# Low parts of the attention's probabilities and of X moved between VectorE and GpSimd, and one accumulating transfer issued later

## The chip, the core and the metric
One core of one Trainium2 chip runs the whole program. The metric is the device time of one execution in microseconds; smaller is better. The core's engines work from queues of their own, each in program order: TensorE (PE; PEld is its weight loads), VectorE (DVE), ScalarE (ACT), GpSimd (POOL) and SyncE (SP), which here only issues transfers.

## What is computed
Attention over 4 x 8 = 32 heads of 768 tokens and 64 columns, with a mask: a query sees only the keys whose six sign bits under a random projection equal its own. Then a mixture of eight experts over the 3072 tokens, each expert taking at most 384.

```python
q_bits = (einsum('bhsd,dk->bhsk', q, proj) > 0); k_bits = ...
mask = q_bucket[:, :, :, None] == k_bucket[:, :, None, :]
scores = np.where(mask, scale * q @ k.T, -1e9)
attn = softmax(scores);  x = attn @ v          # [4*768, 8*64]
logits = x @ w_gate                            # greedy assignment, cap N // E
out[mask_e] = np.maximum(x[mask_e] @ w1[e], 0.0) @ w2[e]
```

## The kernel before
Products run on 16-bit operands. A number is therefore split into a high part (a cast) and a low part (the number minus its high part), and a product is the sum of three: high x high, high x low, low x high. Much of the work beside TensorE is making these low parts.

The 32 heads come in eight groups of four (h = 4G + j). A group's q, k and v are loaded at once (L77). ScalarE casts the high parts (`cast`). For groups 3 to 7 the low part of q and k is made by ScalarE writing the negated high part (`turn`, L152) and a GpSimd transfer that adds the f32 original from DRAM to it (`adds`, L154). SP then moves the parts into the operand tiles QA, KA, QB, KB (`moves`, L200, signs L206).

The main loop runs over steps t, six for each head (one for each block of 128 keys), and in each step emits its parts in the order of `ORD='SF0r1LRA'`: S the score passes of a head some twelve steps ahead, for its row maxima (TensorE L267, VectorE reduction L269); F the last key block's product with v and the quotient `norm` (L353 to L357, tile X); 0 and 1 the two halves of a block's scores and exponentials (`ST`, TensorE L316 and L317, ScalarE L318, tile pt); L the low part of the probabilities of the step before (`lo`, L322 for one block, L325 for two at once); A the product with v (`AV`, L339 to L341); r and R whatever was put by `add(n, ...)` on half-step n = 2t (r) or 2t + 1 (R). The product `AV` of block s of head h stands four steps behind its scores (`LAG=4`).

Who makes `lo` is chosen by head: `E0` for head 0, `E1` for head 1, else the list of the head in `EL`, else `PAT[h % 2]`. A number below 6 in the list gives that block to VectorE; 10, 11 or 12 gives the first, second or third pair of blocks to VectorE as one instruction (11: third and fourth key block). All else goes to GpSimd.

When two heads (an odd h and the one before) are done, their 128 columns X are stored as f16 high and low parts (tile XS): `xhigh` on ScalarE (L365) at half-step 12h + 23, `xlow` (L367) four half-steps later, that is in step 6h + 13, the second step of head h + 2, behind that step's `lo`. `xlow` also calls `xout`, which issues on SP a turning transfer XS to XT (L377) and one to x_dram (L378).

Other work with a fixed place: v's high part by ScalarE and low part `vl` by VectorE (`sv`, L221, two instructions in steps 4 and 5 of the second head of a group); a head's maxima are copied by VectorE (`m_four`, L277, at the end of a step), turned by TensorE two steps later (`m_turn`, L282), rectified by ScalarE (tile mr) and put into QA by a transfer on ScalarE's queue (`m_lay`, L287, qa<-mr), which the head's scores L316 need. TensorE's L231 sums v for the rows that no key matches.

`Z4` holds the half-steps of groups 4 to 7 relative to 48(G - 1): four `turn` (q, k, q, k) and then the two `adds` (q, k).

Of the kernel before, what the change touches and what calls it, by code (L numbers as in the profile page):

```python
# [15 lines left out]
PS = bass.MemoryType.PSUM  # L16
DR = bass.MemoryType.DRAM

AP=dict(PAT=[[11], []],
 ORD='SF0r1LRA',  # L20
 LAG=4,
 VM=[2, 2, 2, 2],
# [2 lines left out]
 E0=[3, 5],  # L25
 E1=[],
 X=[5, 4, 20, 15],
 XE=0,
 MR=3,
 MT=4,  # L30
 LEAD=[9,12,40,4],
# [9 lines left out]
 MS=74,  # L41
 BS=3,
 Z3=[77,85,88,91,93,97],
 Z4=[-20,-12,-18,-9,-15,-6],
 EA=[262, 32, 5],
 EG={2: 0, 3: 3},
 MO=['', 'AKs', 'BqL', 'lmk', 'c|ABqKLslmk', 'ABKLsq|cklm', 'ABKLsq|cklm'],
# [4 lines left out]
 OPS='i2 b0 t0 w6 r0 r2 k1 l0 l1 s0 r1 s1 c0 s2 P0 c1 g0 B0 D0 d0 u0 u1 f0 w2 s3 t1 C0 C1 m0 v0 e0 s4 w2 e1 s5 w2 e2 m1 r3 r5 l3 l2 v1 v2 s6 s7 | s8 | x0 | w0 | x1 s9 | r4 s10 | | | s11 m2 v3 | x3 | | x2 | m3 | | | | | |')  # L52
PAT,E0,E1,DW,LEAD=(AP[k] for k in ('PAT','E0','E1','DW','LEAD'))
NB=dict(S=2,T=3,V=1)
HK=385
EMPTY=60000.0
def attention(tc, nc, ctx, qT, kT, vv, proj, wg, x_dram, L, jp, identf, ident, B, late=None, after=None):
    S=768; NG=2*B; NH=8*B; LAG=AP['LAG']
    cp=ctx.enter_context(tc.tile_pool(name="cp",bufs=1))
# [4 lines left out]
    V=nc.vector; A=nc.scalar; G_=nc.gpsimd; T=nc.tensor; SY=nc.sync  # L64
# [129 lines left out]
    def moves(G,part=0):  # L194
# [15 lines left out]
        todo=dict(A=(go,QA,h[0]),B=(go,QB,h[0]),K=(go,KA,h[1]),L=(go,KB,h[1],64),s=(signs_,),c=(clear,G),q=(nxt,0),k=(nxt,1),l=(go,KB,l[1]),m=(go,QB,l[0],64))  # L210
        for x in AP['MO'][part] if G==1 else AP['MO'][min(G+2,6)].split('|')[part]:
            f,*x=todo[x]; f(*x)
# [134 lines left out]
    X={}; XS={}; normed=set(); turned={}  # L347
# [54 lines left out]
    def add(n,f,*a):  # L402
        if n>=2*(6*NH+LAG+6): raise ValueError('an operation has no step')
        at.setdefault(n,[]).append((f,a))
# [8 lines left out]
    n=-1; early=[]  # L413
    for o in AP['OPS'].split():
        if o=='|': n+=1
        elif n<0: OPS[o[0]](int(o[1:]))
        else: add(n,OPS[o[0]],int(o[1:]))
        if o[0]=='e': early.append(int(o[1:]))
    add(AP['WS'],wsplit); add(AP['SU'],sumv,0)
    for G in range(1,NG):  # L420
        p=AP['P1'] if G==1 else AP['P2'] if G==2 else AP['P3'] if G==3 else [48*(G-1)+x for x in AP['P4']]
        st,sg=(AP['P4'] if G>3 else p)[16:18]
# [3 lines left out]
        for n in range(4):  # L426
            if G<3: add(p[8+n],sub,G,n%2,n//2)
            else:
                z=AP['Z3'] if G==3 else [48*(G-1)+x for x in AP['Z4']]
                add(z[n],turn,G,n%2,n//2)  # L430
# [7 lines left out]
        for j in range(4):  # L438
            n=48*(G-1)+AP['CV'][j] if G>3 else p[15]+st*j
# [13 lines left out]
    for h in range(1,NH,2):  # L453
        b,d=h//8,h%8//2; n=2*(6*h+5+LAG)+AP['X'][0]
        if h==NH-1: n=2*(6*h+5+AP['LL'][5])
        if h==NH-1:
            for c in (0,3): add(n,xpart,4*b+d,1,c,c+3)
            for hf in range(2): add(n+AP['X'][1]*hf,xtr,b,d,hf)
            add(n+4,logits,b,[d]); add(n-5,xpart,4*b+d,0)
            add(n,xout,4*b+d,False)  # L460
        else:
            add(n,xhigh,4*b+d); add(n+AP['X'][1],xlow,4*b+d,(V,G_)[AP['XE']])
        if h==NH-1: pass
        elif b==B-1: add(n+AP['X'][3],logits,b,[d])
        elif d==3: add(n+AP['X'][2],logits,b,range(4))
        if after and d==3 and b in AP['EG']:
            for i,f in enumerate(after(AP['EG'][b],b,lambda: psT.tile([128,512],F32,name="pst"),lambda: psV.tile([128,512],F32,name="psv"))):
                add(n+5 if b==B-1 else max(n+AP['X'][2]+3,AP['EA'][0]+AP['EA'][1]*b)+AP['EA'][2]*i,f)
    for n,f in enumerate(late or ()):
        a,d=AP['LT'] if n<3 else AP['L0']  # L470
# [529 lines left out]
@with_exitstack  # L1000
def tile_bucket_attention_moe(ctx, tc, qT, kT, vv, proj, wg, w1, w2, out):
    nc = tc.nc
    B = qT.shape[0] // 2
    drp = ctx.enter_context(tc.tile_pool(name="drp", bufs=1, space=DR))
    x_dram = drp.tile([768 * B, 1024], F16, name="x_dram")
    M = Moe(tc, nc, ctx, 768 * B)
    late = M.consts()
    with ExitStack() as c1:
        c1.enter_context(tc.manual_schedule())
        attention(tc, nc, c1, qT, kT, vv, proj, wg, x_dram, M.Lm, M.jp, M.identf, M.ident, B, late, M.early)  # L1010
    with ExitStack() as c2:
        M.open(c2, x_dram, w1, w2, out)
        with tc.manual_schedule():
            M.start()
            M.run()
# [34 lines left out]
```

## Time and profile before
| | us |
|---|---|
| median of 3 runs | 702.49 |
| lowest and highest | 700.73, 705.22 |
| the profiled execution | 705.62 |
| its span, first to last instruction | 703.8 |

The profiled execution is one of its own; its rows are times inside the span. The attention fills the first 376 us or so, the routing and the experts the rest. In the rows, "out<-in" are the tiles written and read, "x" is a count, and a wait is put down to what ended it.

### The profile page before, as it was taken

To read this page: it belongs to the slowest core of one execution; us is meant where nothing else is said; L and a number is where in the kernel's file an instruction comes from. 1 tells how busy PE (TensorE), PEld (TensorE's weight loads), DVE (VectorE), ACT (ScalarE), POOL (GpSimd) and SP (SyncE) were. 2 spreads that over 40 slices of the span, in tenths; PEclk is the share of its full clock that TensorE was granted. 3 is DMA by queue.
4 is the path that set the end of the run, shared out by engine and by line. 5 is a ranking of instruction groups with operands and counts; after the bars stand their busy time and mean duration, and the time that the engine had idled before them with its cause. 6 is when DMAs were issued, how large, how long until landed. Compare 5 with 4: busy or idle time off the path is not lost. (4 is left out here: it accounts for less than half of the span.)

```text
span 703.8 us, 19016 instructions
## 1 busy us (share of the span) xinstructions
PE 656.3 (93%) x7761; PEld 420.3 (60%) x7769; DVE 525.7 (75%) x1226; ACT 393.8 (56%) x805; POOL 508.6 (72%) x464
## 2 busy tenths in 40 slices
PE   9899999899998999999996699999999999999994
PEld 2566676667666677677775565555555555555551
DVE  5879898778879779798887849798979797923110
ACT  5767787676777868765571253617171625353620
POOL 7599888777798678867840453858787878787751
PEclk9999999999999999999997599999999999999998
DMA  9539867778987789861122444353544445263501
GB/s 224 149 108 196 214 185 132 183 135 155 223 132 178 137 154 226 138 143 14 45 54 56 129 158 165 135 195 136 182 148 152 163 135 195 89 256 127 203 31 45
DMA packets 64300, 102.55 MB, mean 146 GB/s; under 512 B 28960, under 2 KB 53588, under 8 KB 62164
## 3 DMA queue, kind: packets, MB, share of 16 engines
q1 hardware_dynamic: 55236, 51.10, 32.0%
q0 software_dynamic: 8224, 50.08, 23.8%
q8 instruction: 61, 1.00, 0.6%
q10 hardware_dynamic: 752, 0.15, 0.1%
q14 instruction: 27, 0.22, 0.1%
HBM read 67.39 MB, written 12.58 MB: 114 GB/s over the span
## 5 line engine op out<-in xcount | busy, mean ns | idle before, releaser
L322 POOL TENSOR_TENSOR lo<-pt 128x768 f16<-128x768 f32 x148 | 245.1, 1674 | 41.9 <-ACT pt L318 37.3
L318 ACT ACTIVATE pt<-pst 128x384 f32<-128x384 f32 x384 | 173.3, 491 | 86.9 <-PE pst L317 82.2
L269 DVE TENSOR_REDUCE m<-pss 128x1 f16<-128x770 f32 x192 | 181.1, 956 | 34.1 <-PE pss L267 33.1
L316 PE MATMUL pst<-qa,ka 128*128 128x384 f16 x384 | 125.2, 326 | 9.4 <-DMA qa<-mr 4.7
L339 PE MATMUL psv<-vh,pt 128*128 128x65 f16 x1152 | 124.8, 195 | 1.6 <-DVE X L357 1.6
L341 PE MATMUL psv<-vh,lo 128*128 128x65 f16 x1152 | 124.6, 194 | 0.8 <-POOL lo L322 0.6
L317 PE MATMUL pst<-qb,kb 128*128 128x384 f16 x384 | 125.2, 326 | 0.0
L340 PE MATMUL psv<-vl,pt 128*128 128x64 f16 x1152 | 124.8, 193 | 0.0
L339 PEld LDWEIGHTS <-pt 128*128 128x128 bf16 x1152 | 107.4, 98 | 18.2 <-DVE X L357 3.7
L340 PEld LDWEIGHTS <-pt 128*128 128x128 bf16 x1152 | 106.2, 99 | 11.0 <-issue 0.2
L867 ACT CAST wh<-wf 128x1024 f16<-128x1024 f32 x64 | 65.4, 1042 | 77.6 <-DMA wf<-in_w_dram,zwidx 56.6
L341 PEld LDWEIGHTS <-lo 128*128 128x128 f16 x1152 | 106.3, 98 | 1.2 <-POOL lo L322 0.9
L267 PE MATMUL pss<-ka,qa 128*128 128x385 f16 x384 | 95.5, 333 | 4.0 <-DVE m L269 2.8
L879 POOL TENSOR_TENSOR wl<-wf,wh 128x512 bf16<-128x512 f32 x74 | 84.1, 1151 | 0.0
L902 PEld LDWEIGHTS <-wh 128*128 128x128 f16 x544 | 50.6, 99 | 30.4 <-issue 0.7
L858 POOL DMA_INDIRECT wf<-in_w_dram,zwidx x20 | 20.0, 998 | 57.2 <-DVE zmi L791 30.6
L914 PEld LDWEIGHTS <-hh 128*128 128x128 f16 x384 | 35.5, 98 | 36.2
L902 PE MATMUL ph<-xx,wh 128*128 128x384 f16 (+1 forms) x304 | 56.9, 313 | 0.0
L316 PEld LDWEIGHTS <-ka 128*128 128x128 f16 x384 | 37.7, 98 | 29.2 <-DMA qa<-mr 6.0
L317 PEld LDWEIGHTS <-kb 128*128 128x128 f16 x384 | 37.4, 97 | 27.4 <-issue 7.1
L902 PE MATMUL po<-xx,wh 128*128 128x384 f16 x240 | 48.1, 326 | 0.0
L989 POOL TENSOR_TENSOR wl<-wf,wh 128x512 bf16<-128x512 f32 x36 | 42.6, 1212 | 4.3 <-ACT wh L867 4.1
(292 smaller groups left out, 1217.6 us busy)
## 6 DMA issues: line engine op xcount, KB each, us to landing
vp<-in_vv_dram SPq DMA_DIRECT2D x8, 768.0 KB
x_dram<-XS SPq DMA_DIRECT2D x16, 384.0 KB
qp<-in_qT_dram SPq DMA_DIRECT2D x7, 768.0 KB
kp<-in_kT_dram SPq DMA_DIRECT2D x7, 768.0 KB
qa<-qh SPq DMA_DIRECT2D x14, 192.0 KB
ka<-kh SPq DMA_DIRECT2D x14, 192.0 KB
qb<-qh SPq DMA_DIRECT2D x14, 192.0 KB
kb<-kh SPq DMA_DIRECT2D x14, 192.0 KB
```

The lines of the kernel that those rows point to most:

```text
L267: T.matmul(ps[:,hf,0:HK],QA[u][:,j,qc*128:qc*128+128],KA[u][:,j,hf*HK:hf*HK+HK],start=True,stop=True)
L269: V.tensor_reduce(M6[h][:,qc:qc+1],ps[:,:,0:HK],axis=AX.XY,op=ALU.max,negate=True)
L316: T.matmul(ps[:,0:384],KA[u][:,j,kr],QA[u][:,j,r],start=True,stop=False)
L317: T.matmul(ps[:,0:384],KB[u][:,j,kr],QB[u][:,j,r],start=False,stop=True)
L318: A.activation(PT[h,kc][0][:,r],ps[:,0:384],AF.Exp,scale=0.125)
L322: eng.tensor_tensor(l,p,p.bitcast(BF)[:,1::2],op=ALU.subtract)
L339: T.matmul(av[:,c,:],ph[:,r],VH[u][:,j,kc,:],start=(kc==0 and c==0),stop=False,skip_group_check=True)
L340: T.matmul(av[:,c,0:64],ph[:,r],VL[u][:,j,kc,:],start=False,stop=False,skip_group_check=True)
L341: T.matmul(av[:,c,:],l[:,r],VH[u][:,j,kc,:],start=False,stop=False,skip_group_check=True)
L867: s.nc.scalar.copy(h[:,r],f[:,r])
L879: for _ in range(n): s.nc.gpsimd.tensor_tensor(*s.pend.pop(0)[1],op=ALU.subtract)
L902: T.matmul(p[:,r],a[:,o:o+128],b[:,d,r],start=n==0 and not c,stop=n==11 and c in (None,2),skip_group_check=c is not None)
```

## The change
Three edits. `PAT` gets the pair of the third and fourth key block also for odd heads (those without a list in `EL`: 9, 11, 13, 15, 17, 19, 21). `XE`, before the index of one engine for all heads (0: VectorE), becomes a range: `xlow` of heads 9 to 25 goes to GpSimd. The fifth number of `Z4`, q's `adds`, goes from -15 to -12.

```diff
-AP=dict(PAT=[[11], []],
+AP=dict(PAT=[[11], [11]],
- XE=0,
+ XE=[9,25],
- Z4=[-20,-12,-18,-9,-15,-6],
+ Z4=[-20,-12,-18,-9,-12,-6],
@@ the attention's list of operations
-            add(n,xhigh,4*b+d); add(n+AP['X'][1],xlow,4*b+d,(V,G_)[AP['XE']])
+            add(n,xhigh,4*b+d); add(n+AP['X'][1],xlow,4*b+d,G_ if AP['XE'][0]<=h<=AP['XE'][1] else V)
```

## Rows read from the trace of the kernel before
**Rows 1.** The page, part 1: busy us (share of the span) xinstructions.
```profile
PE 656.3 (93%) x7761; PEld 420.3 (60%) x7769; DVE 525.7 (75%) x1226; ACT 393.8 (56%) x805; POOL 508.6 (72%) x464
```
**Rows 2.** Stretches: length, each engine's busy us (x), granted clock, DMA share, GB/s.
```profile
120.00:130.00 10.00, 7.91 (x122) 5.67 (x119) 7.60 (x11) 5.07 (x12) 6.31 (x7) 0.95 0.79 156
130.00:140.00 10.00, 10.00 (x138) 7.14 (x137) 8.04 (x10) 7.23 (x18) 7.18 (x7) 0.87 0.80 213
...
130.00:345.00 215.00, 206.10 (x3258) 149.69 (x3257) 181.28 (x247) 153.47 (x356) 170.49 (x131) 0.99 0.76 148
```
**Rows 3.** Waits, 130 to 345 us: us in total, times, longest.
```profile
POOL lo L322 <- ACT pt L318: 28.0, 27, 3.0
...
POOL ql L154 <- ACT ql L152: 13.5, 4, 4.3
...
PE pst L316 <- ACT pt L318: 3.7, 4, 0.9
...
PE pst L316 <- DMA qa<-mr: 2.6, 2, 1.5
...
PE psv L339 <- DVE X L357: 1.4, 4, 0.4
...
PE pst L282 <- DVE m L277: 0.6, 2, 0.4
```
**Rows 4.** Timeline of GpSimd in head 10: start, us, instruction, [idle before <-releaser].
```profile
148.52 0.88 POOL L154 DMA_DIRECT2D ql<-in_qT_dram  x1 [2.77 <-ACT ql L152]
...
150.27 3.97 POOL L322 TENSOR_TENSOR lo<-pt 128x768 f16<-128x768 f32 x2 [0.75 <-ACT pt L318]
```
**Rows 5.** Instructions of tiles lo and XS: duration ns min/median/max, first and last start.
```profile
L322 POOL TENSOR_TENSOR lo<-pt x148: 1455/1467/3085, 28.4 to 360.2; 128x768 f16<-128x768 f32 x148
L325 DVE TENSOR_TENSOR lo<-pt x16: 1745/1748/2937, 54.7 to 369.6; 128x1536 f16<-128x1536 f32 x16
...
L367 DVE TENSOR_TENSOR XS<-X,XS x15: 946/1047/2254, 62.0 to 366.1; 128x768 f16<-128x768 f32 x15
```
**Rows 6.** Timeline of VectorE in head 17.
```profile
219.48 2.20 DVE L367 TENSOR_TENSOR XS<-X,XS 128x768 f16<-128x768 f32 x1
...
223.34 0.15 DVE L353 TENSOR_SCALAR r<-psv 128x6 f32<-128x6 f32 x1
...
225.09 1.64 DVE L221 TENSOR_TENSOR vl<-vp,vh 128x768 f16<-128x768 f32 x1
...
228.79 0.15 DVE L277 COPY m<-m 128x18 f16<-128x18 f16 x1
```
**Rows 7.** Timeline of TensorE: heads 8 and 9, head 17, head 21.
```profile
128.23 0.34 PE L316 MATMUL pst<-qa,ka 128*128 128x384 f16 x1 [2.09 <-DMA qa<-mr]
...
141.63 0.23 PE L282 MATMUL pst<-ident,m 128*128 128x128 f16 x1 [0.40 <-DVE m L277]
...
222.05 0.35 PE L346 MATMUL psv<-wf,qa 128*128 128x65 f16 x6
...
224.36 0.20 PE L339 MATMUL psv<-vh,pt 128*128 128x65 f16 x1 [0.34 <-DVE X L357]
...
228.42 0.34 PE L316 MATMUL pst<-qa,ka 128*128 128x384 f16 x1 [1.49 <-DMA qa<-mr]
...
230.29 0.22 PE L282 MATMUL pst<-ident,m 128*128 128x128 f16 x1
...
274.25 0.23 PE L282 MATMUL pst<-ident,m 128*128 128x128 f16 x1 [0.21 <-DVE m L277]
```
**Rows 8.** Timeline of SP, the next group's moves in head 11.
```profile
159.86 3.58 SPq L200 DMA_DIRECT2D qa<-qh  x2
163.49 1.28 SPq L200 DMA_DIRECT2D qb<-qh  x2
```
**Rows 9.** Timeline of VectorE in head 9.
```profile
137.30 2.06 DVE L221 TENSOR_TENSOR vl<-vp,vh 128x768 f16<-128x768 f32 x1
```

## Prediction
> **What bounds the kernel now.** Read the page's busy table first: TensorE works 93% of the span and no other engine more than 75% [rows 1]. The table by stretches says where the change can act: its edits touch heads 9 to 27, which run from about 130 to 345 us, and there TensorE is busy 206.1 of 215.0 us [rows 2]. So 8.9 us is all that could be won; the routing and expert stages behind 345 us only move along. The waits of that stretch then name the 8.9 us [rows 3]: 3.7 us of scores waiting for ScalarE's exponentials, 2.6 for the small transfer of a head's maxima (qa<-mr), 1.4 for VectorE's quotient X, 0.6 for VectorE's copy of maxima (L277); the rest is shorter. GpSimd's two large waits, 28.0 us for exponentials and 13.5 for q's negated part, are idle time of an engine that TensorE hardly waits for: no wait of TensorE for GpSimd's lo stands in that list. The reader is to see that GpSimd has room, that VectorE is the engine that holds TensorE up in the odd heads, and that little is at stake.
>
> **The later adding transfer.** `adds` for q moves from half-step -15 to -12, in groups 4 to 7 only: four transfers. It passes one thing on GpSimd's queue, the `lo` of an even head's fifth block. GpSimd stood 2.77 us for ScalarE's ql, then issued the transfer, and the `lo` behind it still waited 0.75 us for its own exponentials [rows 4]. So that `lo` can't start sooner than 150.27 us; the wait is renamed, not removed. The transfer's issue (0.88 us) now falls between two `lo`. What hides it: the sixth block's product comes three steps later. Its landing moves some 3 to 4 us, and the transfer that reads it is issued ten steps on, some 18 us (a step is about 1.8 us: 215 us for some 20 heads of six steps). Cost 0; with the cover gone it would be 4 x 0.88 = 3.5 us. That POOL's wait of 13.5 us shrinks in the after-profile while TensorE gains nothing from it is what I expect to see.
>
> **The low part of X on GpSimd.** Nine `xlow` (heads 9, 11, ... 25) leave VectorE. A single one takes 0.946 us when it meets nothing and up to 2.254 us; GpSimd's `lo` of the same shape (128x768) 1.455 to 3.085, median 1.467 [rows 5]. The spread shows that the two engines hold each other up when both subtract from SBUF. For an `xlow` on GpSimd I take 1.47 us, the nearest row: 13.2 us more there. Against it stand 14 `lo` that leave (20.5 us), so GpSimd ends 7.3 us lighter.
> Where VectorE's relief matters is the second head of each group (13, 17, 21, 25; 9 keeps its `xlow`, since that is head 7's). In head 17 `xlow` holds VectorE 2.20 us, and the quotient is begun at 223.34 [rows 6] although TensorE's last product of the head ended at 222.05 + 0.35 = 222.40 [rows 7]. So 0.9 of the 2.20 us reaches the quotient, and TensorE's wait for X of 0.34 goes; four such waits, 1.4 us in all [rows 3, 7].
> But in heads 13 and 17 the next thing that is late is not VectorE: 4 us on, TensorE waits 1.49 us for the maxima's transfer [rows 7] (two waits, 2.6 us [rows 3]). That transfer was issued well before and lands when it lands; a TensorE that arrives 0.34 earlier waits 0.34 longer. Gain there: 0. In head 21 the same kind of gain runs into the wait below. Only head 25 keeps it: -0.34.
> On SP's queue the turning transfer of `xout` now waits for GpSimd. In the fourth head of a group GpSimd is later with it than VectorE was, by some 3 us (one `lo` and the q transfer are ahead of it). Behind it on SP stand the next group's moves; the first two took 3.58 us where the next two took 1.28 [rows 8], so the second waited some 2 us for the scores of the old group, and that takes the delay up. Cost 0, at worst 1 us on a queue whose data the next group's first score passes read some eleven steps later.
>
> **The third and fourth block's low part on VectorE.** `PAT` now gives odd heads 9 to 21 what even heads have (heads 1 to 7 and 23 to 31 have lists of their own): seven paired subtractions of 1.748 us [rows 5], 12.2 us. Over the stretch VectorE thus swaps nine `xlow` for seven pairs and stays equally full. The place decides. In the fourth head of a group (11, 15, 19) there is idle time behind every reduction as in the even heads, whose pairs stand at the same step; no TensorE wait for a VectorE `lo` is in the list. Cost 0.
> In the second head (9, 13, 17, 21) the pair falls between two `vl` subtractions, ahead of the second `vl` and the copy L277, and TensorE's transpose L282 two steps later can't start before that copy. In-order queue: reduction, `vl`, pair, reduction, `vl`, copy. Now the sum, head by head, from the copy's end:
> Head 9: the first `vl` took 2.06 us [rows 9]; its likely partner on GpSimd, the `lo` of the third and fourth block, is gone, so 0.95 (the shape's undisturbed time [rows 5]). +1.75 - 1.11 = +0.64. TensorE already waits 0.40 there [rows 7]: +0.6.
> Heads 13 and 17: -0.9 (from `xlow`), -0.7 (`vl` 1.64 to 0.95), +1.75 = +0.15. The copy ended at 228.94 and L282 started at 230.29 [rows 6, 7]: room of 1.35. Cost 0.
> Head 21: the same +0.15, but here L282 already waits [rows 7], and the 0.4 won at X is given back: +0.2 on the old time.
> Head 25: no pair. -0.34.
> Sum: 0.6 + 0 + 0 + 0.2 - 0.34 = about +0.5 us. Bounds: from below, all that hangs on these waits goes, 1.4 + 0.6 + 2.6 = 4.6 us won [rows 3]. From above, each pair in the second heads first waits for one whole GpSimd subtraction, 1.47: 2 x 1.47 in heads 9 and 21, and 0.15 + 1.47 - 1.35 = 0.3 each in 13 and 17 if both have head 17's room: +3.5, with the sum +4.0. I take the middle case, since GpSimd, freed of the third and fourth `lo`, should be idle when the pair starts.
> The row shows 2.20 us for a subtraction that takes 0.946 alone [rows 5, 6]. The Trainium skill (SBUF — State Buffer, Who interferes with whom) says a VectorE instruction with two SBUF inputs and a GpSimd one that reads SBUF exclude each other and the second waits until the first is through; the trace's numbers fit that, and by it alone the sum would lie anywhere from +0.5 to +4.0, as the engines happen to meet.
>
> **Rivals.**
> *Both engines meet.* GpSimd is not idle when the pairs start: +4.0, 706.5 us. For it: the pairs' own maximum, 2.937 against 1.748 [rows 5]. Against: most were at the median. The Trainium skill (Perfetto Trace Analysis, Optimizing Scalar/DVE Operations) warns that moving work between VectorE and GpSimd might not help because of the shared port; the spread in rows 5 is in line with it.
> *The relief gets through.* The maxima's transfers land earlier with the shifted traffic, and the copies come in time: -4.6, 697.9 us. For it: the list counts only two such waits of the matmul in four groups [rows 3], so two groups do without. Against: the loads ahead of these transfers stay where they are.
> *The pairs are late in all seven heads.* TensorE reaches the third block's product before the pair is through, and each costs its whole 1.75: +12.2, 714.7 us, slower by over 1%. It decides where a pair starts more than about half a microsecond later than in an even head. Against: the even heads' pairs show no wait.
> *The clock falls once more.* The wait of 1.49 us in head 17 grows to 1.8. The one longer wait, 2.09 us [rows 7], is followed by a granted clock of 0.95 and 0.87 in two stretches of 10 us [rows 2]: part of the time at the lower of the two levels (1.2 instead of 2.4 GHz), 1.8 us lost. Two more such falls and the sum: +4.1, 706.6 us.
> That the change does nothing that can be measured is inside my forecast.
>
> **How the numbers follow.** The profiled execution took 705.62 us, 703.8 of it span; by the sum it would be 706.1. The median of the three runs is 702.49, 3.1 below that one execution, so the forecast is 702.5 + 0.5 = 703.0 us. Chances: forecast 0.58, relief 0.16, engines meet 0.12, clock 0.08, late pairs 0.04, something faster still 0.02. The range 699.0 to 707.0 takes in the forecast, both prices near 706.5 and half of the relief; outside lie the rest of the relief, the late pairs and strays, about 0.2. 1% is 7.0 us, about what a measurement of this kernel can tell from no change: below 695.5 I put 0.03, above 709.5 0.05, between 0.92.
>
> **What would show it.** Right: GpSimd's wait for ql gone, its wait for exponentials longer; TensorE's waits for X gone in heads 13 to 25; a longer wait of L282 for L277 in heads 9 and 21; the wait for qa<-mr 0.3 longer in 13 and 17; TensorE busy about 206 us over the same 215. Wrong: a TensorE wait for VectorE's `lo` (late pairs), `vl` and pairs above 2 us (engines meet), a second stretch of lower clock, or waits for qa<-mr that vanish.

## The result and the profile after

| | before | after |
|---|---|---|
| median, both measured in turn on one chip (us) | 702.25 | 706.89 |
| lowest and highest of 20 runs each (us) | 697.78, 708.5 | 703.82, 710.41 |
| span of the profiled execution (us) | 703.8 | 708.3 |

The changed kernel takes 1.0064 times as long, with a 95% interval of 1.0041 to 1.0087: 4.5 us lost, inside the forecast range (699 to 707) and near its upper end, 3.9 us above the forecast of 703.0.

Where the 4.5 us are shows best between marks that both traces have: the starts of the quotients (L353) of heads 8, 24, 28 and 31. The table by stretches, the kernel before first (columns as in [rows 2]):

```profile
135.55:311.11 175.56, 167.19 (x2630) 120.56 (x2629) 147.04 (x197) 130.97 (x303) 141.65 (x112) 1.00 0.85 163
311.11:352.41 41.30, 40.39 (x674) 30.43 (x672) 36.80 (x57) 23.67 (x55) 32.49 (x21) 1.00 0.31 55
352.41:374.45 22.04, 21.69 (x427) 17.03 (x425) 18.37 (x28) 14.21 (x33) 8.22 (x8) 1.00 0.26 64
```
and the changed kernel:
```profile
134.16:312.60 178.44, 167.72 (x2626) 120.83 (x2625) 148.41 (x196) 130.30 (x301) 132.33 (x104) 1.00 0.80 155
312.60:355.57 42.97, 41.50 (x678) 31.06 (x677) 37.80 (x55) 24.36 (x56) 36.84 (x23) 1.00 0.30 63
355.57:377.62 22.05, 21.70 (x427) 17.05 (x426) 18.38 (x28) 14.21 (x33) 8.23 (x8) 1.00 0.27 64
```
The three stretches together are 238.90 us before and 243.46 after: +4.56, as much as the timed difference. Of it +2.88 lies in heads 9 to 24, where TensorE's idle time (length less busy) goes from 8.37 to 10.72, and +1.67 in heads 25 to 28. (The time up to head 8's quotient, 128 to 136 us, differs between executions of one kernel, so whole spans are not compared here.)

The quotient is a mark on VectorE, and in the kernel before it came late in heads 12, 16, 20 and 24, behind `xlow`. The last products of head 24 on TensorE, the kernel before first:
```profile
309.82 0.35 PE L346 MATMUL psv<-wf,qa 128*128 128x65 f16 x6
```
```profile
312.06 0.35 PE L346 MATMUL psv<-wf,qa 128*128 128x65 f16 x6
```
They end 0.94 us before the quotient (310.17, 311.11), and in the changed kernel 0.19 before it (312.41, 312.60). So the table counts 0.75 us of the loss one stretch too late. Measured from the end of one head's last product (L346) to that of the next, only these heads differ by more than 0.05 us: 9 (+1.83), 12 (+0.23), 13 (+0.23), 17 (-0.14), 21 (+1.47), 25 (-0.51) and 27 (+1.44), together +4.55. The second heads of the groups, 9, 13, 17 and 21, have 3.39 of it.

The waits of 130 to 345 us in the changed kernel, the lines that answer to [rows 3]:

```profile
POOL lo L322 <- ACT pt L318: 53.1, 25, 5.8
...
PE pst L316 <- ACT pt L318: 4.5, 5, 0.9
PEld L282 <- DVE m L277: 4.2, 5, 0.9
...
PE pst L282 <- ACT pt L318: 2.1, 4, 0.6
...
PE psv L341 <- DVE lo L325: 1.6, 2, 1.0
...
PE pst L316 <- DMA qa<-mr: 1.4, 1, 1.4
PE pss L267 <- DVE m L269: 1.4, 5, 0.4
```
TensorE's four waits for X and GpSimd's 13.5 us for ql are gone. New are waits of TensorE for VectorE's `lo`, and L282 now waits 0.53 to 0.55 us in all four second heads, where it waited in heads 9 and 21 alone (0.40 and 0.21 [rows 7]). The list puts these down to ScalarE's pt, but that is not what ended them: in head 21 VectorE's copy L277 ends at 276.28 + 0.15 = 276.43 and L282 starts at 276.48.

In what follows a line is given the head whose scores are made at that time; that head's quotient comes four steps after its last scores. VectorE in head 21 of the changed kernel, then GpSimd, then TensorE's waits (timelines: start, us, instruction, [idle before <-releaser]):

```profile
270.30 0.95 DVE L221 TENSOR_TENSOR vl<-vp,vh 128x768 f16<-128x768 f32 x1
271.17 3.02 DVE L325 TENSOR_TENSOR lo<-pt 128x1536 f16<-128x1536 f32 x1
274.11 0.95 DVE L269 TENSOR_REDUCE m<-pss 128x1 f16<-128x770 f32 x1
274.98 1.37 DVE L221 TENSOR_TENSOR vl<-vp,vh 128x768 f16<-128x768 f32 x1
276.28 0.15 DVE L277 COPY m<-m 128x18 f16<-128x18 f16 x1
```
```profile
270.84 1.74 POOL L322 TENSOR_TENSOR lo<-pt 128x768 f16<-128x768 f32 x1 [0.83 <-ACT pt L318]
```
```profile
273.67 0.32 PE L316 MATMUL pst<-qa,ka 128*128 128x384 f16 x1 [0.83 <-ACT pt L318]
...
275.12 0.49 PE L267 MATMUL pss<-ka,qa 128*128 128x385 f16 x2 [0.21 <-DVE m L269]
...
276.48 0.23 PE L282 MATMUL pst<-ident,m 128*128 128x128 f16 x1 [0.55 <-ACT pt L318]
```
GpSimd begins the fifth block's `lo` at 270.84, 0.33 us before the pair. That `lo` ends at 272.58, and the pair, 1.75 us of work, ends at 274.19: it did its work only as GpSimd came to its end. The pairs of heads 9, 13 and 17 look the same (3.02, 3.05, 3.02 us), though in head 13 GpSimd is ahead by no more than 0.04 us; those of heads 11, 15 and 19 take 1.75.

At head 27, in the kernel before: VectorE, then GpSimd.

```profile
333.41 0.30 DVE L618 TENSOR_TENSOR zeq<-Lm,zm 128x144 f32<-128x144 f32 x1
...
334.50 0.95 DVE L322 TENSOR_TENSOR lo<-pt 128x768 f16<-128x768 f32 x1
```
```profile
334.75 2.02 POOL L322 TENSOR_TENSOR lo<-pt 128x768 f16<-128x768 f32 x1 [1.43 <-ACT pt L318]
```
In the changed kernel: VectorE, GpSimd, and the TensorE waits behind them.
```profile
335.21 0.90 DVE L618 TENSOR_TENSOR zeq<-Lm,zm 128x144 f32<-128x144 f32 x1
...
336.90 1.86 DVE L322 TENSOR_TENSOR lo<-pt 128x768 f16<-128x768 f32 x1
```
```profile
333.05 2.89 POOL L322 TENSOR_TENSOR lo<-pt 128x768 f16<-128x768 f32 x2
336.48 5.03 POOL L322 TENSOR_TENSOR lo<-pt 128x768 f16<-128x768 f32 x3 [0.54 <-ACT pt L318]
```
```profile
339.69 0.49 PE L267 MATMUL pss<-ka,qa 128*128 128x385 f16 x2 [0.39 <-DVE m L269]
...
340.75 0.29 PE L396 MATMUL pss<-wgs,XT 128*128 128x16 f16 x6 [0.20 <-DVE m L269]
...
342.46 0.49 PE L267 MATMUL pss<-ka,qa 128*128 128x385 f16 x2 [0.38 <-DVE m L269]
```
Before, GpSimd was idle when `zeq`, a small instruction of the routing, ran on VectorE, and VectorE's `lo` began 0.25 us ahead of GpSimd's: TensorE waited for neither. Now X's low part of head 25 stands on GpSimd and makes its next two `lo` late; the second of them runs beside `zeq`, which takes 0.90 us instead of 0.30. That puts VectorE's `lo` 0.42 us behind the following `lo` of GpSimd, and it takes 1.86 instead of 0.95. The two are 1.51 us longer together, and head 27 is 1.44.

### The profile page after: what moved, and what is told of

It is laid out like the page before. It is cut to its first block, busy times and chain, and to the rows that moved or that the text cites. A ratio compares the mean times of both kernels' runs of the same rounds, so it can differ in the third digit from the quotient of the medians.

```text
span 708.3 us, 19023 instructions
## 1 busy us (share of the span) xinstructions
PE 652.7 (92%) x7769; PEld 420.2 (59%) x7769; DVE 528.6 (75%) x1224; ACT 394.1 (56%) x805; POOL 503.5 (71%) x459
## 5 line engine op out<-in xcount | busy, mean ns | idle before, releaser
L322 POOL TENSOR_TENSOR lo<-pt 128x768 f16<-128x768 f32 x134 | 228.4, 1748 | 68.1 <-ACT pt L318 62.7
L316 PE MATMUL pst<-qa,ka 128*128 128x384 f16 x384 | 125.6, 327 | 11.3 <-ACT pt L318 5.7
L879 POOL TENSOR_TENSOR wl<-wf,wh 128x512 bf16<-128x512 f32 x74 | 84.1, 1151 | 0.2 <-issue 0.2
L316 PEld LDWEIGHTS <-ka 128*128 128x128 f16 x384 | 37.8, 98 | 29.2 <-DMA qa<-mr 5.9
L325 DVE TENSOR_TENSOR lo<-pt 128x1536 f16<-128x1536 f32 x23 | 46.6, 2027 | 2.5 <-ACT pt L318 2.4
```

The costliest lines, as they stand in the source:

```text
L316: T.matmul(ps[:,0:384],KA[u][:,j,kr],QA[u][:,j,r],start=True,stop=False)
L322: eng.tensor_tensor(l,p,p.bitcast(BF)[:,1::2],op=ALU.subtract)
L879: for _ in range(n): s.nc.gpsimd.tensor_tensor(*s.pend.pop(0)[1],op=ALU.subtract)
```

## The experiments

Eleven kernels were run. Ratio: to the kernel before, timed on the same chip, with its 95% interval. The three other columns come from each kernel's profiled execution, between the marks above: heads 9 to 24 (quotient 8 to quotient 24), TensorE's idle time in it, heads 25 to 28. The length of heads 9 to 31 in one execution agrees with the timed difference to about 2.5 us (3.1 in e10). In five of the profiled executions besides e3's, part of heads 9 to 24 ran at a lower granted clock: it is 0.97 there in e1 and 0.99 in e6, e7, e8 and e10, where the others have 1.00. In e1 three heads have it, and TensorE's busy time is 172.4 us instead of 167.2, so one such fall adds about 1.7 us to the lengths of the table (an estimate from these two numbers).

| kernel | ratio | 9 to 24, us | idle, us | 25 to 28, us |
|---|---|---|---|---|
| before | 1 | 175.56 | 8.37 | 41.30 |
| whole change | 1.0064 [1.0041, 1.0087] | 178.44 | 10.72 | 42.97 |
| e1 pairs alone | 1.0150 [1.0108, 1.0192] | 188.01 | 15.60 | 41.29 |
| e2 X's low part alone | 1.0051 [1.0017, 1.0085] | 175.63 | 8.74 | 42.98 |
| e3 later transfer alone | 1.0269 [1.0223, 1.0315] | 195.38 | 19.99 | 41.30 |
| e4 whole, without the meeting | 1.0045 [1.0015, 1.0075] | 176.95 | 9.85 | 42.98 |
| e5 whole, without pairs | 1.0069 [1.0042, 1.0096] | 176.27 | 9.36 | 42.98 |
| e6 whole, pairs in heads 11, 15, 19 | 1.0047 [1.0020, 1.0074] | 177.97 | 9.25 | 42.98 |
| e7 e5, X of 9 to 23, turns later by two | 0.9993 [0.9969, 1.0017] | 175.62 | 7.68 | 41.53 |
| e8 whole, without the later transfer | 1.0117 [1.0073, 1.0161] | 180.29 | 12.01 | 42.98 |
| e9 e3 with a gap on GpSimd | 1.0004 [0.9975, 1.0033] | 174.86 | 7.33 | 41.29 |
| e10 whole, other pair in second heads | 1.0084 [1.0056, 1.0113] | 176.36 | 8.72 | 43.26 |
| e11 as e7, turns later by one | 1.0002 [0.9973, 1.0031] | 174.51 | 8.49 | 41.53 |

### Each part alone (e1, e2, e3)

e1, the kernel before with the pairs:
```diff
- PAT=[[11], []]
+ PAT=[[11], [11]]
```


> The paired subtractions of the odd heads alone (seven pairs on VectorE); X's low part stays on VectorE, q's adding transfer at its old place. Theory A (the loss is the pair of a group's second head, which is issued just after GpSimd has begun the low part of the fifth block and waits for it; 3.0 us where 1.75 is its own time): the loss is here, 2 to 6 us above before, all of it in the intervals of heads 9, 13, 17 and 21, nothing in 11, 15 and 19. Theory B (no meeting is needed: VectorE's queue between two vl subtractions is simply too long by a pair of 1.75 us): 3 to 5 us above before, and the pairs themselves mostly at 1.75. Theory C (the loss comes with X's low part on GpSimd): within 1 us of before.

The pairs of heads 9, 13, 17 and 21 take 3.01 to 3.02 us here too, and with X's low part still on VectorE TensorE waits 5.0 us in three of these heads for the pair itself:
```profile
PE psv L341 <- DVE lo L325: 5.0, 3, 2.7
```
All four heads are longer, and heads 11, 15 and 19 are not: the place is Theory A's, but the loss, 10.5 us by the ratio, is well above its 2 to 6. About 5 us of the longer heads are the lower clock in heads 9, 13 and 21 (granted 0.88 to 0.89).

e2, the kernel before with X's low part of heads 9 to 25 on GpSimd:
```diff
- XE=0
+ XE=[9,25]
```


> X's low part of heads 9 to 25 on GpSimd alone; no pairs in odd heads, q's adding transfer at its old place. Theory A and B: the quotients of heads 12, 16, 20 and 24 come 0.5 to 0.8 us earlier, of which part is lost again to the transfers of the maxima; some 1.2 us are lost in heads 26 and 27, where GpSimd now runs later beside VectorE's subtractions; in all 0 to 2 us below before. Theory C: 2 to 5 us above before, as the whole change.

The waits for X go, and TensorE's waits for qa<-mr in heads 13 and 17 [rows 3] go too. Yet nothing is won: heads 25 to 28 lose 1.68 us, and in heads 10, 14, 18 and 22 a new wait appears on ScalarE. Its `turn` of the next group's q finds the tile ql still being read by the last group's transfer to QB. ScalarE in head 14:
```profile
184.28 0.84 ACT L152 ACTIVATE ql<-qh 128x768 f16<-128x768 f16 x1 [1.36 <-DMA qb<-ql]
```
Behind it on ScalarE stand the exponentials, for which TensorE then waits: the line PE pst L316 <- ACT pt has 6.3 us in ten waits, where it had 3.7 in four [rows 3]. So X's low part alone, at 3.6 us by its ratio, loses nearly what the whole change loses, as Theory C has it. In the trace the second heads gain by it (by the ends of TensorE's last products they take 45.2 us together instead of 49.1), the heads behind them give it back, and head 27 loses 1.44.

e3, the kernel before with the fifth number of `Z4` at -12:
```diff
- Z4=[-20,-12,-18,-9,-15,-6]
+ Z4=[-20,-12,-18,-9,-12,-6]
```


> q's adding transfer at -12 alone. All theories: within 1 us of before. GpSimd's wait for ScalarE's ql of 13.5 us in 130 to 345 us is gone and its wait for exponentials is larger by 10 us or more; the intervals of heads 9 to 27 as before within 0.3 us, apart from the waits for the maxima's transfers.

This is the largest miss of the study: 18.8 us lost by an edit that was costed at nothing. VectorE in heads 10 and 11, then GpSimd, then TensorE:
```profile
153.41 6.88 DVE L367 TENSOR_TENSOR XS<-X,XS 128x768 f16<-128x768 f32 x1
```
```profile
151.87 0.88 POOL L154 DMA_DIRECT2D ql<-in_qT_dram  x1
152.48 1.77 POOL L322 TENSOR_TENSOR lo<-pt 128x768 f16<-128x768 f32 x1
153.89 0.40 POOL L554 MEMSET us<- 128x1 bf16 x1
153.95 3.17 POOL L322 TENSOR_TENSOR lo<-pt 128x768 f16<-128x768 f32 x2
156.78 1.18 POOL L154 DMA_DIRECT2D kl<-in_kT_dram  x1
157.39 2.07 POOL L322 TENSOR_TENSOR lo<-pt 128x768 f16<-128x768 f32 x1
```
```profile
161.22 0.80 PE L267 MATMUL pss<-ka,qa 128*128 128x385 f16 x2 [3.35 <-DVE m L269]
```
VectorE's subtraction of 0.95 us starts while GpSimd is at work and ends at 160.29, one subtraction after GpSimd's stream has ended (157.39 + 2.07 = 159.46). It got no turn at the boundaries between GpSimd's instructions, nor during the issue of k's transfer or a memset of 128x1 elements that stand among them. TensorE then waited 3.32 to 3.40 us, four times, and about these waits the clock fell: the granted clock of heads 9 to 24 is 0.96 where it was 1.00, so part of the stretch ran at 1.2 instead of 2.4 GHz, and TensorE's busy time there is 175.39 us instead of 167.19 (heads 9 to 24 of e3; columns as in [rows 2]):
```profile
134.62:330.00 195.38, 175.39 (x2630) 124.99 (x2629) 170.51 (x197) 131.44 (x303) 139.68 (x112) 0.96 0.74 150
```
In the kernel before, GpSimd stood still for want of exponentials in just this place, and VectorE's subtraction slipped in (VectorE, then GpSimd, head 11 of the kernel before):
```profile
154.30 0.95 DVE L367 TENSOR_TENSOR XS<-X,XS 128x768 f16<-128x768 f32 x1
```
```profile
154.76 3.23 POOL L322 TENSOR_TENSOR lo<-pt 128x768 f16<-128x768 f32 x2 [0.49 <-ACT pt L318]
```

### What held the subtraction (e9)

e3, with GpSimd's low part of the second key block in heads 11, 15, 19 and 23 replaced by a memset, which leaves that low part out of the result:
```diff
+            elif ss==1 and hh in (11,15,19,23): G_.memset(PT[hh,ss][1],0.0)
             else: lo(hh,ss,V if ss in on else G_)
```


> The later adding transfer alone (no pairs, X's low part all on VectorE), with one subtraction of GpSimd in heads 11, 15, 19 and 23 left out: the low part of the second key block is set to zero by a memset (0.73 us) instead, so the low part of these probabilities is missing. The two adding transfers stay where they were, among GpSimd's subtractions. With the later transfer alone, VectorE's low part of X took 6.9 us in these heads and TensorE then waited 3.35 us four times. Theory S (a VectorE subtraction of two SBUF tiles gets no turn as long as GpSimd's subtractions follow one another without a gap; the transfers matter only because they fill the gap): the memset is a gap, so X's low part takes 2 to 3.5 us there, TensorE's waits for the copy of maxima L269 are under 2 us in all, and the time is within 3 us of the kernel before, ratio 0.998 to 1.006. Theory T (the issue of the adding transfers itself holds VectorE up): X's low part still takes over 5 us, until k's transfer is issued, and the ratio stays above 1.02.

VectorE, then GpSimd, in head 11 of e9:
```profile
148.17 3.12 DVE L367 TENSOR_TENSOR XS<-X,XS 128x768 f16<-128x768 f32 x1
```
```profile
148.71 1.75 POOL L322 TENSOR_TENSOR lo<-pt 128x768 f16<-128x768 f32 x1
150.12 1.03 POOL L497 MEMSET lo<- 128x768 f16 x1
150.80 1.19 POOL L154 DMA_DIRECT2D kl<-in_kT_dram  x1
151.41 2.08 POOL L322 TENSOR_TENSOR lo<-pt 128x768 f16<-128x768 f32 x1
```
The subtraction ends at 151.29, 0.83 us after the `lo` before the memset: it ran during the memset. The 3.35 us waits are gone, and the ratio is 1.0004. So Theory S holds: what counts is a run of GpSimd subtractions without such a gap, not the transfers as such, which stand where they stood in e3. One memset in each of four heads gave back 18 us.

### The second heads' pairs (e4, e5, e6, e10)

e4, the whole change, but GpSimd's low part of the fifth block in heads 9, 13, 17 and 21 is a memset, which leaves that low part out of the result, so that the pair meets nothing:
```diff
+            elif ss==4 and hh in (9,13,17,21): G_.memset(PT[hh,ss][1],0.0)
             else: lo(hh,ss,V if ss in on else G_)
```


> The changed kernel, but in heads 9, 13, 17 and 21 GpSimd fills the low part of the fifth block with zeros instead of subtracting (an instruction that reads nothing from SBUF); the low part of those four blocks is left out of the result. VectorE's and TensorE's work is the same. Theory A: the pairs of these heads take 1.75 us instead of 3.02, the interval from the quotient of a group's first head to that of its second falls from 13.1 to 11.0 to 12.3 us, and the time falls by 2 to 4 us against the changed kernel, to 703 to 705. Theory B: the pairs' length doesn't matter, the intervals stay above 12.8 and the time within 1 us of 706.9.

All four pairs take 1.75 us now, and TensorE's waits for VectorE's `lo` are gone. VectorE in head 21:
```profile
263.21 1.75 DVE L325 TENSOR_TENSOR lo<-pt 128x1536 f16<-128x1536 f32 x1
```
That it was the fifth block's `lo` that the pair waited for is shown by this. TensorE's gaps from the quotient of head 8, 12, 16 and 20 on, up to L282 and the L231 behind it, add up to 6.92 us in the whole change and to 3.99 here: the meeting costs 2.9 us there. By the ends of TensorE's last products the four second heads take 52.5 us in the whole change, 49.0 here and 49.1 before. But the heads behind them (10, 14, 18, 22) take 53.4 us instead of 50.7, TensorE's idle time over heads 9 to 24 falls by 0.87 us alone, and the timed ratios lie too close to be told apart: ScalarE's turn waits for qb<-ql again (4.2 us), as in e2.

e5, the whole change without pairs:
```diff
- PAT=[[11], [11]]
+ PAT=[[11], []]
```


> The whole change without its seven pairs: GpSimd keeps X's low part of heads 9 to 25 and q's later adding transfer. By the intervals between the quotients of successive heads, X's low part alone left heads 9 to 25 0.6 us and the heads behind them 1.2 us longer than before. Theory A (the second heads' pairs are what makes the whole change slower; the later transfer costs nothing once X's low part is no longer VectorE's): second heads at 11.1 to 11.6 us instead of 13.1, but heads 10, 14, 18 and 22 longer again, so within 1 us of the run with X's low part alone, ratio 1.003 to 1.006 to the kernel before. Theory D (the later transfer costs of itself, as the 3.35 us waits in the run with it alone): four long waits of TensorE for the copy of maxima L269, ratio above 1.015. Theory E (ScalarE's turn of q waits for the transfer of q's low part of the group before, and that gives the gain back): waits of L152 for qb<-ql of some 5 us in four heads, as with X's low part alone.

```profile
PE pst L316 <- ACT pt L318: 6.4, 10, 1.1
...
ACT ql L152 <- DMA qb<-ql: 5.5, 4, 1.8
```
No faster than the whole change. TensorE's gaps after the four quotients, 6.92 us in the whole change and 3.99 in e4, are 2.10 here. The later transfer does no harm here, since X's low part has left VectorE (against Theory D). The wait of ScalarE's turn, 0.3 us in the whole change, is 5.5 here (Theory E): with the pairs TensorE comes later and that transfer is nearly always through, without them it isn't.

e6, the pairs in the fourth heads only (empty lists in `EL` for 9, 13, 17, 21):
```diff
- EL={..., 7: [5], 23: [], ...}
+ EL={..., 7: [5], 9: [], 13: [], 17: [], 21: [], 23: [], ...}
```


> The whole change with the pairs in heads 11, 15 and 19 alone: in heads 9, 13, 17 and 21 GpSimd keeps all six low parts. Theory A (the pairs of the second heads cost 1.8 us each, those of the fourth heads nothing): second heads at 11.1 to 11.6 us, heads 11, 15 and 19 at 9.1 to 9.4 as before; the same time as without any pair, within 1 us. Theory B (VectorE is simply too full, wherever a pair stands): between the run without pairs and the whole change, heads 11, 15 and 19 or the heads behind them longer by over 0.5 us each.

Heads 11, 15 and 19 take 9.16, 9.38 and 9.37 us between quotients, as without pairs: the fourth heads' pairs cost nothing. The second heads are at 11.28, 11.79, 11.35 and 11.13. The timed ratio is below e5's and the whole change's and apart from neither.

e10, the whole change with the first pair of blocks in the second heads:
```diff
- EL={..., 7: [5], 23: [], ...}
+ EL={..., 7: [5], 9: [10], 13: [10], 17: [10], 21: [10], 23: [], ...}
```


> The whole change, but in heads 9, 13, 17 and 21 VectorE's pair is the first and second key block instead of the third and fourth: as much work on VectorE, two steps earlier, ahead of the subtractions of v's low part, and at the same time GpSimd has nothing to subtract. Theory A (the loss comes from the place: the pair meets GpSimd's fifth block and stands between v's low parts): the pairs take 1.75 us, TensorE's wait for VectorE's lo and the longer wait for the copy of maxima go, TensorE's idle time from the quotient of head 8 to that of head 24 is 8.5 to 9.5 us instead of 10.7; ratio 1.001 to 1.005. Theory B (VectorE is too full in these heads wherever the pair stands): second heads at 13 us as in the whole change, idle time 10.5 us or more, ratio 1.006 to 1.010.

In the trace the place decides: every pair takes 1.75 us, and TensorE's idle time is 8.72. By quotients the second heads take 10.83 to 10.91 us, but the pair now stands right ahead of the first of these quotients and makes it late; by TensorE's last products they take 11.85 to 12.01, where the whole change has 13.11 to 13.14. And TensorE's waits for X are back:
```profile
PE psv L339 <- DVE X L357: 2.3, 4, 0.8
```
And the timed ratio, 1.0084, is above what Theory A gave. The profiled execution, 2.8 us longer than before in heads 9 to 31 (with a stretch of lower clock in head 18), does not show where the timed 5.9 come from; that stays open.

### Undoing one part, and a version meant to be better (e8, e7, e11)

e8, the whole change with q's transfer where it was:
```diff
- Z4=[-20,-12,-18,-9,-12,-6]
+ Z4=[-20,-12,-18,-9,-15,-6]
```


> The whole change with q's adding transfer where it was (-15): pairs in seven heads and X's low part of heads 9 to 25 on GpSimd. Theory A (the later transfer is neutral once X's low part is GpSimd's): second heads at 13.1, within 1.5 us of the whole change, ratio 1.005 to 1.008. Theory D (the later transfer costs of itself): faster than the whole change by over 2 us, ratio under 1.004. Theory G (the later transfer is what pays for the pairs, by keeping GpSimd from standing in front of them): slower than the whole change by over 2 us, GpSimd's wait for ScalarE's ql back at 12 to 18 us and X's low part later, ratio above 1.01.

Slower than the whole change by the medians, with intervals that overlap a little: the later transfer, which loses 18.8 us when it stands alone, does no harm here and perhaps some good. TensorE waits for the pair in all four second heads (4.2 us, where the whole change has 1.6), but heads 13, 17 and 21 take as long as in the whole change (13.10 to 13.11 us). Head 9 is longer, 14.50 instead of 13.10, at a granted clock of 0.88. There the pair itself takes 1.74 us and TensorE waits 1.33 for it all the same: the `vl` ahead of it in VectorE's queue met GpSimd instead (2.17 us, where 0.95 is its own time). Where the rest of the timed difference lies was not settled.

e7, X's low part of heads 9 to 23 on GpSimd, the later transfer, no pairs, and ScalarE's two turns of q later:
```diff
- PAT=[[11], [11]]   XE=[9,25]   Z4=[-20,-12,-18,-9,-12,-6]
+ PAT=[[11], []]     XE=[9,23]   Z4=[-18,-12,-16,-9,-12,-6]
```


> X's low part of heads 9 to 23 by GpSimd and q's later adding transfer, no pairs, and ScalarE's two turns of q two half-steps later (first and third number of Z4: -18 and -16 instead of -20 and -18). Theory E (the gain of X's low part is given back in heads 10, 14, 18 and 22, because ScalarE's turn of q waits there for the transfer of the group before, 5.6 us in four waits, and the exponentials behind it are late): the wait of L152 for qb<-ql under 1 us in all, heads 10, 14, 18 and 22 at 12.2 to 13.4 as before, heads 26 and 27 at 10.13 and 9.71; 3 to 5 us below the run without pairs, ratio 0.994 to 0.998: faster than both kernels. Rival F (TensorE, arriving earlier, would wait in these heads for ScalarE's exponentials in any case): heads 10, 14, 18 and 22 stay 0.7 to 2.1 longer than before, ratio 1.001 to 1.004.

e11, the same with
```diff
- Z4=[-18,-12,-16,-9,-12,-6]
+ Z4=[-19,-12,-17,-9,-12,-6]
```


> X's low part of heads 9 to 23 by GpSimd, no pairs, q's adding transfer later, and ScalarE's turns of q one half-step later than in the kernel before (two in the run e7, where they fell next to the cast of X's high part and heads 14 and 22 waited 1.3 us for exponentials). Theory E (ScalarE's wait for qb<-ql is what gave the gain back): the wait of L152 is 0 to 1.5 us in all, heads 26 and 27 as before, ratio 0.994 to 0.999. Rival F (TensorE waits for ScalarE's exponentials in heads 10, 14, 18 and 22 in any case): TensorE's idle time from head 8 to head 24 is 8 us or more, ratio 0.999 to 1.003.

In e7 ScalarE's wait for qb<-ql is gone, head 27 is back at 9.71 us (11.15 in e5), and the ratio falls from e5's 1.0069 to 0.9993, intervals apart. So these two together are what X's low part on GpSimd costs when no pair is there. The profiles put 1.45 us on heads 25 to 28 and 0.65 on heads 9 to 24, out of 5.3 timed; e7's has a stretch of lower clock in head 10 (16.17 us, where e11 takes 13.43), which hides a part. e11 measures the same as e7, with one such wait of 1.3 us left. Neither beats the kernel before. TensorE's idle time in heads 9 to 24 stays at 7.7 and 8.5 us, by other waits: in heads 14 and 22 of e7 TensorE waits 1.3 us for exponentials where the kernel before waits 0.93, and e11 has a wait of 2.00 us for X's turning transfer, which the kernel before has not. Rival F is not excluded.

## Why the forecast was right, and where it was not

Its total was in the range, but not by its own sum. The sum was +0.5 us; measured was +4.5. The rival *Both engines meet* gave +4.0 at a chance of 0.12, and it is the one that came about. By the forecast's own signs of being wrong, three of four are there: TensorE waits for VectorE's `lo`, pairs take over 2 us, and the waits for qa<-mr in heads 13 and 17 are gone. TensorE is busy 203.2 us in 130 to 345 us, where 206 was forecast. Step by step:

- **The later transfer, cost 0.** Right for the whole change: GpSimd's 13.5 us of waiting for ql vanished, its waiting for exponentials rose from 28.0 to 53.1, and no wait of TensorE hangs on it in the trace (e8 leaves open whether it gained something). But the reason given was too narrow. It looked at GpSimd's own queue and the transfer's readers. What was to be seen as well was that GpSimd's standing still is VectorE's chance to subtract: alone, this edit costs 18.8 us (e3, e9). It was harmless here only because another part of the same change had taken X's low part off VectorE.
- **X's low part in heads 13, 17 and 21.** The waits for X went, as said. That a TensorE 0.34 us earlier would wait 0.34 longer for qa<-mr was wrong: with X's low part alone (e2) those two waits are gone. Why they go no run shows. The gain came and was lost again one head further on, at ScalarE's turn, which the forecast never looked at.
- **Head 25, -0.34.** Right at its place: the wait for X went, and head 25 is 0.51 us shorter by TensorE's last products. What the sum left out, at nothing and without a reason, is head 27, two heads on: +1.44. Head 27 has a list of its own, with the fourth block on VectorE, and GpSimd, later by one `xlow`, now subtracts at the same time, first beside `zeq` (0.90 us instead of 0.30) and then beside that `lo` (1.86 instead of 0.95). e7 and e11, without head 25's edit, have 41.53 us in heads 25 to 28 instead of 42.98. An `xlow` on GpSimd took 1.645 to 1.934 us, median 1.649, where 1.47 was taken.
- **Pairs in the fourth heads, 0.** Right: three of 1.75 us, no wait (e6).
- **Pairs in the second heads, +0.8 in all.** This is the step that failed: "GpSimd, freed of the third and fourth `lo`, should be idle when the pair starts". It was idle until 0.33 us before (0.04 in head 13). Freed of two blocks it stood waiting for the fifth block's exponentials, which came first. Each pair took 3.02 us or a little more, 1.27 above its work. The gaps of TensorE as added up for e4 come to 4.67 us before and 6.92 after. By head: 0.39 to 1.95 in head 9, 1.66 to 1.68 in 13, 2.01 to 1.71 in 17, 0.61 to 1.58 in 21. The places of the cost, heads 9 and 21, and the cover in 13 and 17 (room of 1.35, [rows 6, 7]) were right; the size, by the lengths of the heads, was +1.83 and +1.47 where +0.6 and +0.2 were taken. Which wait is named differs (qa<-mr in head 9, VectorE's `lo` in 13 and 17, exponentials in 21), since several things come due at once and the list names the last; what the four heads share is the pair's length and, 0.5 us each, the late copy L277.
- **Head 12, +0.23.** Not in the sum, and not settled.

The rival's +4.0 was therefore near the result partly by luck: by it the four second heads cost 4.3 us (0.8 + 3.5), and they cost 3.39; head 27, which it had not, made up for that. Nor does the meeting by itself explain why the change is slower: without it (e4) and without the pairs (e5) the kernel is not clearly faster, since what the second heads then win is given back at ScalarE's turn, and head 27's loss stays. Of the other rivals, *pairs late in all seven heads* is excluded by heads 11, 15 and 19, and *the clock falls once more* by the granted clock of 1.00 over heads 9 to 24. The waits for qa<-mr that *The relief gets through* wanted gone do go in e2, but no time is won by it.

By their ratios the parts cost 10.5, 3.6 and 18.8 us alone (e1, e2, e3: ratio less 1, times the 699.43 us that the kernel before took beside them), and 4.5 together. The Trainium skill (SBUF — State Buffer, Who interferes with whom) states that the engine that issues first gets the shared ports for its whole instruction, while the other blocks fully. The pairs agree with it: 0.04 to 0.33 us late, they waited for one GpSimd instruction. The 6.88 us of e3 go beyond it: there VectorE was held up over four GpSimd subtractions, one that was running and three that started after it. The measurement decides: the price of a meeting is not bounded by one instruction.

## What to carry to other kernels

Before an idle stretch of GpSimd is closed, look at what VectorE does in it: a subtraction of two SBUF tiles may live on that gap, and without it, as in e3, wait until GpSimd's whole run of such instructions is through. When work is moved off an engine to relieve it, read both queues at the new place and ask which instruction starts first, within tenths of a microsecond; being lighter on average says nothing about that. And when an early arrival is the gain, follow it to the next resource that is late (here a single tile still being read by a transfer), for that is where it is given back.

## What the runs showed of the hardware

- A VectorE subtraction from two SBUF tiles that takes 0.95 us alone took up to 6.96 us beside GpSimd subtractions that followed one another without a gap, and ended 0.82 to 0.83 us after the last of them (e3). A GpSimd memset of 128x768 elements in the run let it through (e9: 3.12 us, of which it waited for the two subtractions ahead of the memset).
- The issue of an adding transfer on GpSimd (1.18 us in the trace) between two GpSimd subtractions was not such a gap in e3, nor was a memset of 128x1 elements (0.40 us).
- In e3 the granted clock over heads 9 to 24 came to 0.96, with four TensorE waits of 3.32 to 3.40 us in the stretch; in the changed kernel, whose waits there are at most 1.43 us, it stayed at 1.00. The longest wait alone does not tell the two apart: e11 had one of 2.00 us in that stretch and stayed at 1.00, and e7 fell in head 10 (0.89), where the longest was 0.99.
